# Attention values of a block's four head pairs in one visit, a new plan of feed-forward items, and a new order at the end

## The chip, the cores and the metric

The program runs on one core of a Trainium2 chip. A core has a matrix engine (TensorE, PE in the profile, with PEld for its weight loads), a vector engine (VectorE, DVE), a scalar engine (ScalarE, ACT), GpSimd (POOL) and a queue for transfers (SyncE, SP). The metric is the device time of one execution in microseconds, the median of several; less is better. The profile is of one execution: its span runs from the first to the last instruction of the program.

## What is computed

Top-32 attention over 8 batches of 8 heads (576 tokens, head size 64), whose output goes token by token into a feed-forward network with the activation h·cos h. All in 32-bit floats, except that the two weight matrices arrive as 64-bit floats.

```python
def _attn_ref(q, k, v):                       # (8, 8, 576, 64) each
    scores = np.matmul(q, k.transpose(0, 1, 3, 2)) / np.sqrt(64)
    kth = np.partition(scores, -32, axis=-1)[..., -32:-31]
    scores = np.where(scores >= kth, scores, -1e9)
    attn = np.exp(scores - np.max(scores, axis=-1, keepdims=True))
    attn = attn / (np.sum(attn, axis=-1, keepdims=True) + 1e-09)
    return np.matmul(attn, v)

x = attn_out.transpose(0, 2, 1, 3).reshape(4608, 512)
h = x @ w_in                                  # (4608, 2048)
out = (h * np.cos(h)) @ w_out                 # (4608, 512)
```

## The kernel before

**Units, slots, blocks.** The 4608 tokens are cut into 36 blocks of 128. A block has four units, one for each pair of heads (`hp` 0 to 3), so there are 144 units. A block that straddles two batches (one in nine) has two `parts`, others one. The main loop has one slot for each unit. In slot i VectorE searches the 32 greatest scores of unit i (L303 to L333: eights found by MAX8, struck out by MATCH_REPLACE8); the later stages of earlier units run beside it.

**A unit's way.** Scores: TensorE, L238, into two PSUM buffers `sc` and, for the last 128 keys, into `rim`; two units' scores are made in every even slot. ScalarE copies them out (`take_scores`, L248 from `sc`, L252 from `rim`). One slot after the search its mask (L381) and exponentials (L389) run on ScalarE, from distances `nd` that VectorE has made early in that slot (L340 to L372; ScalarE takes them up at L379). A slot later GpSimd parts the words into halves (`split`, L412, L414), SyncE writes them to DRAM (L440) and reads them back transposed into a `pT` buffer (L446; three buffers). Two slots later still come the values, P@V: `values` (L450) multiplies `pT` with v on TensorE, the last 64 keys first (tails, `v_tail`), into 128 columns of each of the two banks of `rim`. VectorE's `take_values` (L467, the instruction is L473) multiplies the result with the reciprocals of the sums into the block's `xT` (five buffers).

**A visit** is one call of `values` with its `take_values`. Before, each even slot visits two units, those of slots i-4 and i-3: a block takes two visits, 18.64 us apart. In the slot, `take_values` stands inside the last round of the search (L330), so VectorE comes to it some eight microseconds into the slot.

**The feed-forward network** is cut into items that `feed` places between the attention's matmuls. Kind 0, first layer (`ff1`): 16 matmul instructions of 128x128 (L522); a block has 8. Two items fill a PSUM bank `mm` (of two), which ScalarE empties with L536 and L538 (`take_first`); two banks make one `g` buffer, and then GpSimd reduces it modulo a period (L558, L567), ScalarE takes the sine (L577; needs another activation table than the exponential: ACT_TABLE_LOAD) and GpSimd multiplies (`gate`, L584). Kind 1, second layer (`ff2`): 4 instructions of 128x512 (L597); a block has 8, all into one bank `o`, which is also one of the two `mm` banks. ScalarE empties it with L607 and sends it out (`take_second`).

**What sets the order.** The order is written out by hand in `slot` (L700): every engine runs its instructions in the order in which they are issued there. `feed` counts ticks, three in each slot, and skips an item that isn't ready: a first-layer item needs the block's four units taken two ticks ago (L618), a second-layer item its gate three ticks ago (L629). `take_banks` is where ScalarE's emptying of full banks enters its queue. In slot 65 of the kernel before, for example: sine, mask, bank of the first layer, exponentials, `take_scores`, and then L607 of block 13; in slot 66 TensorE's first item is that of block 14 that opens the bank which L607 emptied. `drain` and `forward` (L751 to L778) do what remains after the last slot. The weights are decoded in the first dozen slots, through staging buffers shared with `g` and `x` (`CHUNKS`, L94).

Of the kernel before, what the change touches and what calls it, by code (L numbers as in the profile page):

```python
# [10 lines left out]
F32 = mybir.dt.float32  # L11
# [6 lines left out]
P = 128  # L18
# [12 lines left out]
def kernel(  # L31
# [9 lines left out]
    nc = tc.nc  # L41
    ctx.enter_context(tc.manual_schedule())
    B, H, D, S = qT.shape
    DM, DF = moe_w_in.shape
    NT = S // P
    TAIL = S - NT * P
    MAIN = NT * P
    NP = H // 2
# [6 lines left out]
    consts = ctx.enter_context(tc.tile_pool(name="consts", bufs=1))  # L55
    loads = ctx.enter_context(tc.tile_pool(name="loads", bufs=6))
    work = ctx.enter_context(tc.tile_pool(name="work", bufs=2))
# [32 lines left out]
    for f in range(NF):  # L90
        w = consts.tile([P, DM], F32, tag=f"w_out{f}", name=f"w_out{f}")
        w_out.append(w)
        chunks.append((moe_w_out[f * P : (f + 1) * P, :], w))
    CHUNKS, XB = 7, 3  # L94
    BUSY = range(8, 11)
    ff = {"live": 0, "tick": 0, "now": 0, "end": False, "kind": 0, "half": 0, "open": 0, "late": False}

# [63 lines left out]
    units = []  # L161
    for t0 in range(0, B * S, P):
        parts = []
        for i, a in enumerate((t0, t0 + TAIL)):
            b, q0 = a // S, a % S
# [7 lines left out]
    pairs = {}  # L173
    v_tails = []
    for i in range(2 * NP):
        t = consts.tile([P, P], F32, tag=f"v_tail{i}", name=f"v_tail{i}")
        nc.gpsimd.memset(t, 0.0)
        v_tails.append(t)

    def place(hp, j):  # L180

        return (hp + j) % 2
# [23 lines left out]
    def load_v(b, hp):  # L206
        st = pairs.setdefault((b, hp), {})
        cols = slice(hp * P, (hp + 1) * P)
        t = loads.tile([P, NT, P], F32, tag="v", name="v")
        nc.sync.dma_start(out=t, in_=v[b, 0:MAIN, cols].rearrange("(c p) e -> p c e", p=P))  # L210
        st["v"] = t

        t = st["v_tail"] = v_tails[b % 2 * NP + hp]
        for j in range(2):
            nc.sync.dma_start(
                out=t[place(hp, j) * TAIL : (place(hp, j) + 1) * TAIL, j * D : (j + 1) * D],
                in_=v[b, MAIN:S, hp * P + j * D : hp * P + (j + 1) * D],
            )

# [200 lines left out]
    def turn(u):  # L420

        s = u.pop("s").rearrange("p j k -> p (j k)")
        pT = u["pT"] = work.tile([P, 2 * NT + 2, P], F32, tag="pT", name="pT", bufs=3)
        for half in range(2):
            tt = ps.tile([P, 512], F32, tag="mm", name="tt", bufs=2)
            for c in range(NT):
                at = (half * NT + c) * P
                nc.tensor.transpose(tt[:, c * P : (c + 1) * P], s[:, at : at + P], ident)
            nc.scalar.copy(out=pT[:, half * NT : (half + 1) * NT], in_=tt.rearrange("p (c q) -> p c q", c=NT))
        at = 2 * NT * P  # L430
        nc.tensor.transpose(room[0][:, P : 2 * P], s[:, at : at + P], ident)
        rden = u.pop("rden")
        for j in range(2):
            lhsT = rden[:, j : j + 1].to_broadcast([P, D])
            nc.tensor.matmul(room[1][j * D : (j + 1) * D, P : 2 * P], lhsT, ident, start=True, stop=True)
        nc.scalar.copy(out=pT[:, 2 * NT :], in_=rim[:, :, 3 * P :])
# [4 lines left out]

    def transposes(u):
        rows = u.pop("rows").rearrange("q h k -> (q h) k")
        pT = u["pT"] = work.tile([P, 2 * NT + 2, P], F32, tag="pT", name="pT", bufs=3)
        words = pT.rearrange("p c q -> p (c q)").bitcast(U16)
        nc.sync.dma_start_transpose(  # L446
            out=words.rearrange("p (c q) -> p c q", c=2 * NT + 2), in_=rows
        )

    def values(us):  # L450


        for b, _, rows, r0 in us[0]["parts"]:
            r = slice(r0, r0 + rows)
            for c in (NT, *range(NT)):
                for i, u in enumerate(us):
                    st = pairs[b, u["hp"]]
                    for j in range(2):
                        d, at = slice(j * D, (j + 1) * D), place(u["hp"], j)
                        if c < NT:  # L460
                            lhsT, rhs = st["v"][:, c, d], u["pT"][:, at * (NT + 1) + c, r]
                        else:
                            t = slice(at * TAIL, (at + 1) * TAIL)
                            lhsT, rhs = st["v_tail"][t, d], u["pT"][t, NT, r]
                        nc.tensor.matmul(room[i][d, r], lhsT, rhs, start=c == NT, stop=c == NT - 1)  # L465

    def take_values(us):  # L467
        blk, hp, n = block_of[us[0]["tok"]], us[0]["hp"], len(us)
        if "xT" not in blk:
            blk["xT"] = work.tile([P, NP, P], F32, tag="xT", name="xT", bufs=5)  # L470
        for i, u in enumerate(us):
            to, o, pT = blk["xT"][:, hp + i], room[i][:, 0:P], u.pop("pT")
            nc.vector.tensor_tensor(out=to, in0=o, in1=pT[:, 2 * NT + 1], op=ALU.mult)  # L473
        blk["left"] -= n
        blk["tick"] = ff["tick"]
# [68 lines left out]
    def take_banks():  # L544
        while full:
            take, *what = full.popleft()
            take(*what)
# [92 lines left out]
    def feed(*kinds):  # L640

        ff["tick"] += 1
        for kind in kinds:
            item(kind)

    def feed_any(n):

        ff["tick"] += 1
        for _ in range(n):
# [11 lines left out]
            else:  # L661
                ff["half"] = 1

    scored, last, last_values = {}, {}, {}
    for i, u in enumerate(units):
        two = i % 2 == 0 and 2 < i
        scored.setdefault(i - 2 if two else i - 1, []).append(u)
        for part in u["parts"]:
            last[part[0], u["hp"]] = i - 2 if two else i - 1
            last_values[part[0], u["hp"]] = i  # L670
    at_slot, at_once = {}, {}

    def load_at(i, *what):
        while i in at_slot:
            i += 1
        at_slot[i] = what

    order = [(b, hp) for b in range(B) for hp in range(NP)]
    for n in range(NP, len(order)):
        i = last[order[n - 6]] if n >= 6 else 0  # L680
        load_at(max(i, 2 * NP + 2), load_qk, *order[n])
        i = last_values[order[n - 6]] if n >= 6 else 0
        load_at(max(i + 4 - i % 2, 2 * NP + 2), load_v, *order[n])

    for hp in range(NP):
        at_once.setdefault(hp // 2 + 2, []).append((load_v, 0, hp))
# [7 lines left out]
    def send(x):  # L694

        split(x)
        write_halves(x)
        transposes(x)

    def slot(i, u, w, x, z):  # L700
        n = (3, 4, 4, 4, 4, 3)[i] if i < NP + 2 else 2
        if i < NP:
            for load, b, hp in at_once[i]:
                load(b, hp)
        load_weights(n, nc.sync if i < NP + 2 else nc.scalar)
        if x:
            (turn if i < NP + 2 else send)(x)
        decoding = i < 3 * NP
        ff["late"] = False
        topk_first(u, w)  # L710
        fold_low(u)
        topk_round(u, 1)
        topk_round(u, 2)
        decode_second(NP)
        decode_third()
        reduce_first()
        reduce_second()
        made = scored.get(i, [])
        if z:
            take_banks()  # L720
        feed(0 if i % 2 else 1)

        for m in made:
            scores(m)
        if z:
            values(z)


        if i % 2 or decoding:
            sines(1)  # L730
        if w:
            mask(w)
        take_banks()
        if w:
            exponentials(w)
        if i + 1 < NU:
            take_scores(units[i + 1])
        topk_round(u, 3, both(w), z)
        ff["late"] = True
        if i in at_slot:  # L740
            load, b, hp = at_slot[i]
            load(b, hp)
        gate(1)
        feed(*((1, 1) if i % 2 else (1,)))
        take_banks()
        decode_first(NP)
        reduce_first()
        reduce_second()
        feed(*((0, 0) if i % 2 else (0,)))

    def forward(n):  # L751
        ff["now"] += 1
# [7 lines left out]

    def drain(w, x, z):

        if x:
            send(x)
        if w:
            merge_first(w)
            merge_second(w)
            bounds(w)
            distances(w)
            mask(w)  # L770
            exponentials(w)
            sums(w)
            reciprocal(w)
        forward(2)
        if z:
            values(z)
            take_values(z)
        forward(2)  # L778
# [10 lines left out]
    for i in range(NU):  # L789
        ff["now"] += 1  # L790
        wq["ready"] = wq["done"]
        u, w, x = (units[i - n] if n <= i else None for n in range(3))
        z = units[i - 4 : i - 2] if i % 2 == 0 and i >= 4 else None
        if NP < i < NP + 3:
            z = units[2:4] if i == NP + 1 else None
        slot(i, u, w, x, z)
    ff["end"], ff["late"] = True, False
    drain(units[NU - 1], units[NU - 2], units[NU - 4 : NU - 2])
    drain(None, units[NU - 1], None)
    drain(None, None, units[NU - 2 : NU])  # L800
# [40 lines left out]
```

## Time and profile before

| | |
|---|---|
| time, median of 3 runs | 1440.79 us (1440.24 to 1440.95) |
| the profiled execution, own time | 1440.46 us |
| its span | 1438.7 us |
| 0 to 119 us (start, weights): VectorE, ScalarE, GpSimd busy | 108.87, 92.82, 81.89 of 119.00 us; TensorE's clock 0.67 |
| 119 to 1368 us (regular slots): VectorE, ScalarE, GpSimd busy | 1233.61, 981.80, 1080.41 of 1249.00 us; TensorE's clock 1.00 |
| 1368 to 1438.7 us (end): TensorE, VectorE, ScalarE busy | 62.97, 12.44, 18.83 of 70.70 us |
| an odd slot, start to start on VectorE | 8.99 us |
| an even slot, with its visit | 9.65 us |
| ScalarE's copy of `rim` (L252) waiting for the values (L465) | 93.6 us in 70 waits, longest 3.6 |
| GpSimd's `halves` (L412) waiting for the exponentials | 149.2 us in 68 waits |
| SyncE's transposes (L446) waiting for the written rows | 415.0 us in 137 waits |
| a transpose, issue to landing | 5.0 us |

The profile names, for each group of instructions, the line of the kernel, engine and operation, what is written from what, and how often; then the busy time, the mean of one in nanoseconds, and the idle time ahead of it with what ended that. A timeline has, instead, start, length, engine, line and operation, and in brackets the idle time ahead. Matmuls overlap, so their distance from start to start is what they cost.

### The profile page before, as it was taken

What the parts mean: (1) busy time and instruction counts of PE and PEld (TensorE: products, weight loads), DVE (VectorE), ACT (ScalarE), POOL (GpSimd) and SP (SyncE); (2) the same over time, 40 slices, a digit from 0 to 9 for tenths busy, and PEclk for the clock granted to TensorE, in tenths of its full rate; (3) what the DMA queues carried; (4) which work ended last, traced back from release to release, by engine and by line L of the source; (5) the groups of instructions that cost most, each with busy time, mean ns of one, the idle gap of its engine ahead of it and who ended that gap; (6) DMA issues with size and microseconds to landing.
All of it is one profiled execution on the core that took longest, in us unless ns stands there. A gap on an engine that the chain in (4) does not pass through costs nothing.

```text
span 1438.7 us, 30312 instructions
## 1 busy us (share of the span) xinstructions
PE 1381.0 (96%) x10304; PEld 986.1 (69%) x10304; DVE 1354.9 (94%) x5235; ACT 1093.5 (76%) x1922; POOL 1166.2 (81%) x812
## 2 busy tenths in 40 slices
PE   5578999999999999999999999999999999999988
PEld 3355777777777777777777777777777777777765
DVE  7999999999999999999999999999999999999921
ACT  6967787778777787778777787777777788778722
POOL 4788888888888888888888888888888888888810
PEclk6679999999999999999999999999999999999999
DMA  9576666556655576556665567556765566655530
GB/s 292 186 199 175 186 195 184 148 159 193 189 159 144 167 185 180 162 146 194 187 171 143 143 182 194 166 154 186 185 173 151 150 162 169 160 147 154 155 81 15
DMA packets 427436, 240.01 MB, mean 167 GB/s; under 512 B 375952, under 2 KB 392592, under 8 KB 427280
## 3 DMA queue, kind: packets, MB, share of 16 engines
q1 hardware_dynamic: 420864, 224.75, 57.3%
q10 hardware_dynamic: 6416, 13.32, 2.6%
q8 instruction: 81, 1.33, 0.4%
q14 instruction: 75, 0.61, 0.2%
HBM read 45.09 MB, written 101.19 MB: 102 GB/s over the span
## 4 chain that ended last, share of the span: by engine, by line
PE 90%; DVE 5%; ACT 3%; DMA 1%; POOL 0%; SPq 0%; issue 0%; POOLq 0%
PE o L597 35%; PE mm L522 34%; PE rim L465 11%; PE sc L238 8%; DVE top L352 2%; PE rim L238 2%; DVE rest L357 1%; DMA st<-in_moe_w_in_dram 1%; ACT st L136 1%; ACT s L389 1%; ACT s L381 0%; ACT w_in L133 0%; DMA pT<-rows 0%; DVE low L357 0%; DVE rest L260 0%; DVE w_out L144 0%
## 5 line engine op out<-in xcount | busy, mean ns | idle before, releaser
L522 PEld LDWEIGHTS mm<-xT,w_in 128*128 128x128 f32 x4608 | 538.8, 193 | 70.8 <-issue 66.6
L522 PE MATMUL mm<-xT,w_in 128*128 128x128 f32 x4608 | 539.9, 276 | 4.0 <-ACT x L538 4.0
L597 PE MATMUL o<-w_out,g 128*128 128x512 f32 x1152 | 537.6, 600 | 6.2 <-POOL g L584 6.2
L352 DVE MAX8 top<-rest 128x8 f32<-128x288 f32 x1152 | 478.7, 451 | 0.0
L412 POOL COPY halves<-s 128x2304 uint16<-128x2304 uint16 x140 | 294.7, 2105 | 149.4 <-ACT s L389 149.2
L357 DVE MATCH_REPLACE8 rest<-top,rest 128x288 f32<-128x288 f32 x864 | 376.3, 443 | 0.0
L597 PEld LDWEIGHTS o<-w_out,g 128*128 128x128 f32 x1152 | 203.1, 191 | 194.4 <-issue 187.5
L352 DVE MAX8 top<-low 128x8 f32<-128x288 f32 x576 | 241.7, 448 | 0.6 <-POOL low L285 0.6
L389 ACT ACTIVATE s<-s,nd 128x576 f32<-128x576 f32 x288 | 220.1, 767 | 0.8
L285 POOL TENSOR_TENSOR low<-low,rest 128x576 int32<-128x576 int32 x141 | 200.3, 1420 | 11.0
L381 ACT ACTIVATE s<-s,top 128x576 f32<-128x576 f32 x288 | 206.2, 766 | 0.0
L276 POOL TENSOR_TENSOR low<-s 128x576 int32<-128x576 int32 x141 | 199.3, 1413 | 5.2 <-ACT s L252 5.2
L536 ACT ACTIVATE g<-mm 128x512 f32<-128x512 f32 x144 | 86.0, 598 | 150.6 <-PE mm L522 150.4
L567 POOL TENSOR_TENSOR x<-g,x 128x1024 f32<-128x1024 f32 x68 | 161.5, 2374 | 5.7
L238 PE MATMUL sc<-k,q 64*128 64x448 f32 (+1 forms) x640 | 149.6, 587 | 12.7 <-DMA k<-in_k_dram 7.0
L584 POOL TENSOR_TENSOR g<-g,x 128x1024 f32<-128x1024 f32 x68 | 160.8, 2365 | 0.0
L465 PE MATMUL rim<-pT,v 128*64 128x128 f32 (+1 forms) x2560 | 147.8, 269 | 0.0
L465 PEld LDWEIGHTS rim<-pT,v 128*64 128x64 f32 x2560 | 129.8, 139 | 12.5 <-issue 11.2
L248 ACT COPY s<-sc 128x896 f32<-128x896 f32 x144 | 128.0, 889 | 4.7 <-PE sc L238 4.7
L252 ACT COPY s<-rim 128x256 f32<-128x256 f32 (+1 forms) x160 | 59.2, 370 | 93.8 <-PE rim L465 93.6
L357 DVE MATCH_REPLACE8 low<-top,low 128x288 f32<-128x288 f32 x288 | 125.4, 443 | 0.0
L260 DVE TENSOR_TENSOR rest<-sc,s 128x576 f32<-128x576 f32 x144 | 107.7, 748 | 7.0 <-ACT s L252 6.5
(55 smaller groups left out, 1215.3 us busy)
## 6 DMA issues: line engine op xcount, KB each, us to landing
rows<-halves SPq DMA_DIRECT2D x140, 640.0 KB, 3.0
out_dram<-ob ACTq DMA_DIRECT2D x36, 256.0 KB, 2.0
q<-in_q_dram SPq DMA_DIRECT2D x31, 288.0 KB, 3.5
st<-in_moe_w_in_dram SPq DMA_DIRECT2D x16, 512.0 KB, 7.0
v<-in_v_dram SPq DMA_DIRECT2D x32, 256.0 KB, 3.3
st<-in_moe_w_out_dram SPq DMA_DIRECT2D x9, 512.0 KB, 4.8
k<-in_k_dram SPq DMA_DIRECT2D x31, 144.0 KB, 3.3
k<-in_k_dram SPq DMA_DIRECT2D x32, 128.0 KB, 3.7
```

The costliest lines, as they stand in the source:

```text
L238: nc.tensor.matmul(to[r0 : r0 + rows, rim_bank(r0, j) if k0 else place(u["hp"], j), 0 : k1 - k0], st["q"][d, q0 : q0 + rows], st["k"][d, k ...
L276: nc.gpsimd.tensor_tensor(out=u["low"].bitcast(I32), in0=s[:, :, 0:HS], in1=s[:, :, HS:S], op=ALU.add)
L285: nc.gpsimd.tensor_tensor(out=low, in0=low, in1=u["rest"][:, :, HS:S].bitcast(I32), op=ALU.subtract)
L352: nc.vector.max(to[:, j], src[:, j])
L357: nc.vector.match_replace(rest[:, j], to[:, j], src[:, j], NEG)
L381: nc.scalar.activation(out=s[:, j], in_=s[:, j], func=AF.Prelu, bias=less[:, j, 1:2], scale=1.0, alpha=FAR)
L389: nc.scalar.activation(out=s[:, j], in_=s[:, j], func=AF.Exp, bias=nd[:, j : j + 1], scale=SCALE, accum_out=den[:, j, 0:1],)
L412: nc.gpsimd.tensor_copy(out=halves[:, :, 0 : 2 * S], in_=s.rearrange("p (k h) -> p h k", h=2))
L465: nc.tensor.matmul(room[i][d, r], lhsT, rhs, start=c == NT, stop=c == NT - 1)
L522: nc.tensor.matmul(mm[:, at : at + w], w_in[f // FC][:, c, (f % FC) * P : (f % FC + 1) * P], blk["xT"][:, c], start=c == 0, stop=c == NC - 1,)
L567: nc.gpsimd.tensor_tensor(out=x, in0=g, in1=x, op=ALU.subtract)
L597: nc.tensor.matmul(o, g[:, at : at + P], w_out[f], start=f == 0, stop=f == NF - 1)
```

## The change

- `values` takes all units of a visit into the two banks of `rim`, unit `hp` into bank `hp % 2` at columns `hp // 2 * 128`, and only the first matmul into each bank half sets `start`.
- `value_slot` says when a unit is visited: all four units of a block in the third slot after the block's last (slots 2 modulo 4), but the first two units of a straddling block two slots earlier; the first block in slot 5. `take_values` takes as many units.
- `pT` has five buffers instead of three, `xT` three instead of five, `CHUNKS` is 6 instead of 7, `v_tail` tiles have 64 columns instead of 128 and aren't cleared.
- Items come from a `plan` by slot modulo 4: 2 in the slot of the visit, then 5, 4 and 5 (before: 3 in even slots, 5 in odd ones).
- Loads of v are placed from the slot of the last visit.
- `drain` begins with `take_banks`, and `ff["half"]` is 1 when the end begins.

```diff
-    CHUNKS, XB = 7, 3
+    CHUNKS, XB = 6, 3
@@
-        t = consts.tile([P, P], F32, tag=f"v_tail{i}", name=f"v_tail{i}")
-        nc.gpsimd.memset(t, 0.0)
-        v_tails.append(t)
+        v_tails.append(consts.tile([P, D], F32, tag=f"v_tail{i}", name=f"v_tail{i}"))
@@
-        pT = u["pT"] = work.tile([P, 2 * NT + 2, P], F32, tag="pT", name="pT", bufs=3)
+        pT = u["pT"] = work.tile([P, 2 * NT + 2, P], F32, tag="pT", name="pT", bufs=5)
@@
+    def place_of(u):
+
+        bank, at = u["hp"] % 2, u["hp"] // 2 * P
+        return bank, room[bank][:, at : at + P]
+
     def values(us):
+        begun = set()
         for b, _, rows, r0 in us[0]["parts"]:
             r = slice(r0, r0 + rows)
             for c in (NT, *range(NT)):
-                for i, u in enumerate(us):
-                    st = pairs[b, u["hp"]]
+                for u in us:
+                    st, (bank, to) = pairs[b, u["hp"]], place_of(u)
...
-                        nc.tensor.matmul(room[i][d, r], lhsT, rhs, start=c == NT, stop=c == NT - 1)
+                        nc.tensor.matmul(
+                            to[d, r], lhsT, rhs, start=(bank, j) not in begun,
+                            stop=c == NT - 1 and u in us[-2:] and r0 + rows == P,
+                        )
+                        begun.add((bank, j))
@@
-            blk["xT"] = work.tile([P, NP, P], F32, tag="xT", name="xT", bufs=5)
+            blk["xT"] = work.tile([P, NP, P], F32, tag="xT", name="xT", bufs=3)
@@
+    def value_slot(i, u):
+
+        if i < NP:
+            return NP + 1
+        return i - i % NP + NP + (0 if len(u["parts"]) == 2 and u["hp"] < 2 else 2)
+
+    valued = {}
+    for i, u in enumerate(units):
+        valued.setdefault(value_slot(i, u), []).append(u)
...
-            last_values[part[0], u["hp"]] = i
+            last_values[part[0], u["hp"]] = value_slot(i, u)
@@
-        load_at(max(i + 4 - i % 2, 2 * NP + 2), load_v, *order[n])
+        load_at(max(i, 2 * NP + 2), load_v, *order[n])
@@
+    plan = (
+        ((0,), (1,), (1, 0)),
+        ((0,), (1, 1), (0, 0)),
+        ((1,), (1,), ()),
+        ((0, 0), (1, 1), (0,)),
+    )
@@
-        feed(0 if i % 2 else 1)
+        feed(*plan[i % NP][0])
@@
-        feed(*((1, 1) if i % 2 else (1,)))
+        feed(*plan[i % NP][1])
@@
-        feed(*((0, 0) if i % 2 else (0,)))
+        feed(*plan[i % NP][2])
@@
     def drain(w, x, z):
 
+        take_banks()
@@
-        z = units[i - 4 : i - 2] if i % 2 == 0 and i >= 4 else None
-        if NP < i < NP + 3:
-            z = units[2:4] if i == NP + 1 else None
+        z = valued.get(i)
         slot(i, u, w, x, z)
-    ff["end"], ff["late"] = True, False
+    ff["end"], ff["late"], ff["half"] = True, False, 1
```

## The prediction

> **What bounds the kernel now.** I read the page's busy shares and its chain of waits first, then TensorE's timeline over one pair of slots, then the same stretch on VectorE and ScalarE, then the last 75 us. Shares and chain (both name TensorE):
>
> ```profile
> PE 1381.0 (96%) x10304; PEld 986.1 (69%) x10304; DVE 1354.9 (94%) x5235; ACT 1093.5 (76%) x1922; POOL 1166.2 (81%) x812
> PE 90%; DVE 5%; ACT 3%; DMA 1%; POOL 0%; SPq 0%; issue 0%; POOLq 0%
> ```
>
> TensorE's timeline of one pair of slots (start, length, line; no idle is noted anywhere):
>
> ```profile
> 703.08 1.98 PE L597 MATMUL o<-w_out,g 128*128 128x512 f32 x4
> 704.90 3.73 PE L522 MATMUL mm<-xT,w_in 128*128 128x128 f32 x32
> 708.48 3.60 PE L597 MATMUL o<-w_out,g 128*128 128x512 f32 x8
> 711.91 3.73 PE L522 MATMUL mm<-xT,w_in 128*128 128x128 f32 x32
> 715.48 1.88 PE L597 MATMUL o<-w_out,g 128*128 128x512 f32 x4
> 717.29 1.02 PE L238 MATMUL sc<-k,q 64*128 64x448 f32 x4
> ...
> 719.44 0.45 PE L465 MATMUL rim<-pT,v_tail 64*64 64x128 f32 x8
> 719.82 1.97 PE L465 MATMUL rim<-pT,v 128*64 128x128 f32 x32
> 721.72 1.98 PE L597 MATMUL o<-w_out,g 128*128 128x512 f32 x4
> ```
>
> From start to start (703.08 to 721.72): 18.64 us a pair. An item of the first layer (16 matmuls of L522) is 1.79 us (3.57 for two), one of the second (4 of L597) 1.72; the scores of two units 2.15 (717.29 to 719.44), the values of two 2.28 (719.44 to 721.72). VectorE and ScalarE beside it:
>
> ```profile
> 703.61 0.49 DVE L473 TENSOR_TENSOR xT<-rim,pT 128x128 f32<-128x128 f32 x2 [0.16 <-ACT s L252]
> ...
> 704.92 0.23 DVE L340 TENSOR_REDUCE top<-top 128x34 f32<-128x68 f32 x1
> ...
> 713.91 0.23 DVE L340 TENSOR_REDUCE top<-top 128x34 f32<-128x68 f32 x1
> ```
>
> ```profile
> 706.82 0.20 ACT L379 ACTIVATE nd<-nd 128x2 f32<-128x2 f32 x1 [0.78 <-DVE nd L372]
> ...
> 708.68 0.60 ACT L536 ACTIVATE g<-mm 128x512 f32<-128x512 f32 x1 [0.32 <-PE mm L522]
> ...
> 713.75 0.60 ACT L607 ACTIVATE ob<-o 128x512 f32<-128x512 f32 x1
> ```
>
> What to see: VectorE has no gap but the 0.16 us ahead of L473, where it waits for ScalarE's rim copy (L252), which waited for the values. L340 opens a slot: an odd slot is 8.99 us, and no slot without a multiply waits anywhere. L607 empties the finished bank of the second layer at 714.35; the next block's first L597 takes that bank at 715.48. So TensorE leads, with 1.1 us in hand at this bank.
>
> **What the Trainium skill says.** "TensorEngine Tiling (Array Packing)", Key Properties: changing the tiling mode drains TensorE. The trace agrees: start to start, single matmuls at the changes (scores to tails, tails to main values, values to L597) are 199 to 202 ns apart on the median, where the values' own steps are 7 or 103. "PSUM — Partial Sum Buffer", section on bank collisions: two engines must not touch one bank in the same 32 partitions, whatever the columns. That is why L252 waits for values that it doesn't read (76.0 us over 58 waits in 200 to 1300 us). "TensorE: Matmul & The Clock Gate": ScalarE's queue is strictly first in, first out; and a pause of some 3.4 us halves TensorE's clock. The trace has the second: after a 4.0 us pause at the end, 32 matmuls take 5.26 us instead of 3.73.
>
> **The change, part by part.** Call V the start of the first L597 after a visit, and a group the 37.27 us of four slots.
>
> *The joined visit.* A visit to two units is 2.28 us: tails 0.18, change 0.20, main 1.70, change 0.20. Four units in one: 2x0.18 + 0.20 + 2x1.70 + 0.20 = 4.16, with the joins 4.2. Two visits were 4.56, so TensorE saves 0.35 us a group, and needs 36.92. Scores straight to L597, and L522 straight to scores, are not in the steady trace; the nearest changes cost 0.1 to 0.2 more than no change, so the saving lies between 0.1 and 0.4. It counts only if nothing else sets the group.
>
> *What the visit does to VectorE's place.* VectorE multiplies (L473) at V+0.53, as now, since L252 stands before it in both. Four multiplies are 0.21 each, so the next slot opens at V + 1.84 + 2x0.21 = V+2.26. Two slots of 8.99 follow: slot 1 of the group (mod 4) opens at V+20.24. Its distances reach ScalarE 1.90 later (704.92 to 706.82): V+22.14.
>
> *ScalarE's queue in that slot.* From L379 to the end of L607 now: 714.35 - 706.82 = 7.53, less the 0.31 that L536 waited for TensorE, 7.22, all of it work in order (mask, bank, table, exponentials, two copies, L607). So the bank is free at V+29.36. ScalarE is there in time for the distances: in slot 0 its work ends about V+18.35, and table and sine end near V+20.8, 1.3 us early.
>
> *TensorE reaches that bank.* Between V and the next block's first L597 the new plan has 7 items of the second layer and 8 of the first: 7x1.72 + 8x1.79 = 26.3; scores once, 2.15; changes 0.3. It is there at V+28.75: 0.6 us too early. Now it is 1.1 late, because two units of values stand between on TensorE and VectorE isn't held until four are done. So TensorE stops 0.6 us, plus 0.05 for the signal and 0.05 to start again (0 to 0.15: after a change the first L597 shows 534 ns instead of 429). Behind it on its queue stand the scores and the values. From that L597 to the next V: 1.81 + 2.15 + 4.2 = 8.17. The loop is 29.36 + 0.10 + 8.17 = 37.63 against 37.27: +0.35 a group. It runs through VectorE, ScalarE and TensorE in turn, so the saved drains don't shorten it.
>
> *Groups.* From V at 123.74 (slot 10) to 1355.99 (slot 142) are 33. Four blocks straddle two batches and touch two groups each: in the first, extra scores in slot 0 fall into the stop (+0.16 rather than +0.35), in the second two units stay in a visit of their own, TensorE is 2.4 us later at the bank and nothing waits (0). 25x0.35 + 4x0.16 = +9.4 us.
>
> *Start.* Slots 4 and 8 lose their multiplies (-0.6 and -1.3 with the 0.86 wait), slot 5 has four units at half clock (about +1.9); slot 10 waits for GpSimd's gate (6.2 us) as before, then its visit is 1.9 longer. Sum +1.9; -1 to +6, as the clock of that visit isn't known. One staging buffer less delays one weight chunk by a slot, in slots that wait for VectorE; the eight memsets (1.2 us of GpSimd) lie before any work.
>
> *End.* Now the loop leaves 12 + 20 items, then 13 + 20; the sum of work is the same. The old order stops here:
>
> ```profile
> 1364.82 3.73 PE L522 MATMUL mm<-xT,w_in 128*128 128x128 f32 x32
> 1372.56 5.26 PE L522 MATMUL mm<-xT,w_in 128*128 128x128 f32 x32 [4.00 <-ACT x L538]
> ```
>
> A first-layer item needs a bank whose emptying is queued on ScalarE behind the last units' mask and exponentials. The new order ends the loop with half a bank filled, fills it and goes on in the open second-layer bank, then has the values. By the same durations no later item waits: the closest is the last half of block 35, gated 0.5 us before its use. Gain 4.0 + 1.5, and 0.1 elsewhere: -5.6 (-6.5 to -3).
>
> *At nothing:* five pT buffers (four units held, one being filled; the fifth slot's transpose is issued after the multiplies); later v loads (3 slots in hand, but one as now at the straddling blocks); transposes before the visit (lands near V+30, tails at V+33.4); three xT buffers (one lives 29 us of 37); GpSimd's gates, due slots later (1.6 us in hand). The first L522 at V+1.82 needs xT, ready at V+1.44; a wait there up to 0.6 is swallowed by the stop.
>
> *Sum* on the profiled span: 1438.7 + 9.4 + 1.9 - 5.6 = 1444.4; outside it lie 1.76 (1440.46 - 1438.7): 1446.2. The median shown is 0.33 above the profiled run: 1446.
>
> **Rivals.**
>
> *A, TensorE still leads (faster).* If the bank comes free by V+28.75, the group is 36.92: 25 x -0.35 and 4 x -0.35, -10; with start and end 1440.8 - 10 + 1.9 - 5.6 = 1427. For: every gap on TensorE now is its own, VectorE needs only 36.87. Against: ScalarE's 7.22 is pure work. It decides from 0.6 us less on the way from V to L607.
>
> *B, the sine falls behind (slower still).* In slot 0 the bank is emptied behind the mask, so GpSimd's reduction, the sine and slot 1's mask move later; 1.3 us in hand. Half a microsecond beyond it goes into every ordinary group: 1446 + 12 = 1458. For: GpSimd is 81% busy. Against: its work fits by the durations.
>
> *C, it cancels.* A stop of only 0.3 us (+0.05 a group) and the full end: 1438 to 1442.
>
> **How the numbers follow.** The bank's loop 68%, own range 1440 to 1454 (0.2 to 0.55 a group, with the bounds of start and end); A 15%; B 10%; C 7%. The range 1436 to 1457 holds the first, C and part of B, and leaves out A and the far part of B. No change means within 0.2% (2.9 us), which is what can be told. Faster by more: A and a little of C, 0.17. Within: most of C and a tenth of the likeliest, 0.15. Slower: 0.68.
>
> **What would show it.** Right: an idle of about 0.6 us before L597 once in four slots, put down to ScalarE L607, and a group of 37.6 us; L473's wait grown to about 0.8. At the end no 4 us stop before L522. Wrong: groups of 36.9 with no wait on L597 (A); L379 waiting for the sine and not for nd (B); or the stop before L522 in slot 3, waiting for xT.

## The result, and the profile after

The changed kernel takes 1444.97 us in the median of ten runs (1443.58 to 1449.18), the kernel before, run beside it, 1440.18 (1439.52 to 1441.36): a ratio of 1.0036, 95% interval 1.0026 to 1.0046. So it is slower by 4.8 us, a third of a percent, outside the scatter of both. The profile is of one of these runs, 1449.18 us, with a span of 1447.4; it is the slowest of the ten, and the part on the start says where its 4.2 us above the median lie.

The page, busy shares and chain of waits:

```profile
PE 1374.4 (95%) x10304; PEld 991.8 (69%) x10304; DVE 1351.3 (93%) x5235; ACT 1088.4 (75%) x1922; POOL 1164.8 (80%) x804
PE 41%; DVE 40%; ACT 14%; DMA 2%; issue 2%; POOL 1%; SPq 0%; ACTq 0%
```

TensorE is busy 6.6 us less than before, and the kernel is slower. (Of the 6.6 us only 1.6 lie in the regular slots, from V of slot 10 to V of slot 142; 3.2 lie before them and 1.7 after.) The second line says why that can be: of the chain that ends last TensorE held 90% before and holds 41% now. The bound is no longer one engine but a loop through three. The chain in order of time, from one visit to the next (start, length, what), shows it whole:

```profile
689.96 2.42 PE rim L469 x44
692.41 0.38 ACT s L250
692.81 0.88 DVE xT L481 x4
...
713.94 0.37 DVE top L350
714.60 1.33 ACT s L379 x2
715.93 0.48 ACT g L544
716.41 0.58 ACT x L546
717.01 1.28 ACT L387
718.42 0.56 issue
718.99 0.94 ACT s L387 x3
719.93 0.79 ACT s L246
720.72 0.27 ACT s L250
720.99 0.51 ACT ob L615
721.63 1.96 PE o L605 x4
...
725.74 4.26 PE rim L469 x80
730.02 0.38 ACT s L250
730.43 0.89 DVE xT L481 x4
```

The values (L469, before the change L465) release the copy of `rim`, and that copy releases the multiplies (L481). VectorE then runs two and a bit slots without a gap; its distances release the mask (L379), ScalarE works through its queue to the emptying of the second layer's bank (its eviction: L615, before the change L607), and that releases TensorE's next second-layer item (L605, before the change L597), behind which the next values stand. From multiply to multiply, 692.81 to 730.43, are 37.62 us.

TensorE's timeline of the same four slots:

```profile
692.29 1.98 PE L605 MATMUL o<-w_out,g 128*128 128x512 f32 x4
...
717.48 3.73 PE L530 MATMUL mm<-xT,w_in 128*128 128x128 f32 x32
721.63 1.96 PE L605 MATMUL o<-w_out,g 128*128 128x512 f32 x4 [0.42 <-ACT ob L615]
...
725.67 0.67 PE L469 MATMUL rim<-pT,v_tail 64*64 64x128 f32 x16
726.26 3.71 PE L469 MATMUL rim<-pT,v 128*64 128x128 f32 x64
729.91 1.98 PE L605 MATMUL o<-w_out,g 128*128 128x512 f32 x4
```

The only idle time is the 0.42 us before L605. From start to start the stop is larger: the two first-layer items before it are over at 717.48 + 3.57 = 721.05, so it is 0.58. The regular slots have 25 such stops, and each ends 0.14 to 0.15 us after the end of the eviction L615. Four of them, in the blocks that straddle two batches, the trace puts down to GpSimd's copy L410, which ended 0.03 to 0.04 us before; there too it is 0.14 us from the eviction. VectorE's side, its multiplies at the end of a visit:

```profile
692.81 0.88 DVE L481 TENSOR_TENSOR xT<-rim,pT 128x128 f32<-128x128 f32 x4 [0.77 <-ACT s L250]
...
730.43 0.69 DVE L481 TENSOR_TENSOR xT<-rim,pT 128x128 f32<-128x128 f32 x3 [0.78 <-ACT s L250]
```

VectorE waits 0.78 us a group there (before, 0.16 us in the pair that the prediction shows), so it is not the bound by its own work.

The span in three, by V (the start of the first second-layer matmul after a visit) in slots 10 and 142:

| | before | after | difference | predicted |
|---|---|---|---|---|
| start, to V of slot 10 | 123.74 | 126.11 | +2.4 (see below) | +1.9 |
| 33 groups, V to V | 1232.25 | 1244.28 | +12.0 | +9.4 |
| end, from V of slot 142 | 82.68 | 76.97 | -5.7 | -5.6 |

### The profile page after: what moved, and what is told of

The parts are those of the page before. It is cut to its first block, busy times and chain, and to the rows that moved or that the text cites. A ratio compares the mean times of both kernels' runs of the same rounds, so it can differ in the third digit from the quotient of the medians.

```text
span 1447.4 us, 30339 instructions
## 1 busy us (share of the span) xinstructions
PE 1374.4 (95%) x10304; PEld 991.8 (69%) x10304; DVE 1351.3 (93%) x5235; ACT 1088.4 (75%) x1922; POOL 1164.8 (80%) x804
## 4 chain that ended last, share of the span: by engine, by line
PE 41%; DVE 40%; ACT 14%; DMA 2%; issue 2%; POOL 1%; SPq 0%; ACTq 0%
DVE top L350 19%; PE o L605 14%; PE rim L469 11%; PE mm L530 10%; DVE rest L355 10%; PE sc L236 5%; DVE rest L258 4%; DVE low L355 3%; ACT s L379 3%; ACT L387 2%; ACT s L387 2%; DVE xT L481 2%; ACT s L246 1%; PE rim L236 1%; ACT s L250 1%
## 5 line engine op out<-in xcount | busy, mean ns | idle before, releaser
L605 PE MATMUL o<-w_out,g 128*128 128x512 f32 x1152 | 534.4, 602 | 24.2 <-POOL g L592 10.5
L410 POOL COPY halves<-s 128x2304 uint16<-128x2304 uint16 x140 | 294.8, 2106 | 102.6 <-ACT s L387 98.7
L605 PEld LDWEIGHTS o<-w_out,g 128*128 128x128 f32 x1152 | 205.2, 190 | 230.2 <-issue 210.8
L379 ACT ACTIVATE s<-s,top 128x576 f32<-128x576 f32 x288 | 205.5, 761 | 0.0
L377 ACT ACTIVATE nd<-nd 128x2 f32<-128x2 f32 x144 | 29.3, 204 | 176.1 <-DVE nd L370 176.0
L469 PE MATMUL rim<-pT,v 128*64 128x128 f32 (+1 forms) x2560 | 140.5, 268 | 0.0
L469 PEld LDWEIGHTS rim<-pT,v 128*64 128x64 f32 x2560 | 130.3, 139 | 6.9 <-issue 5.8
```

Of the source, the lines that this page charges most:

```text
L379: nc.scalar.activation(out=s[:, j], in_=s[:, j], func=AF.Prelu, bias=less[:, j, 1:2], scale=1.0, alpha=FAR)
L410: nc.gpsimd.tensor_copy(out=halves[:, :, 0 : 2 * S], in_=s.rearrange("p (k h) -> p h k", h=2))
L469: nc.tensor.matmul(to[d, r], lhsT, rhs, start=(bank, j) not in begun, stop=c == NT - 1 and u in us[-2:] and r0 + rows == P,)
L605: nc.tensor.matmul(o, g[:, at : at + P], w_out[f], start=f == 0, stop=f == NF - 1)
```

## The experiments

Theory: the loop of the bank, as in the prediction. Rivals: VectorE's longer wait at the joined visit sets the group; the uneven plan of items does; ScalarE has simply more to do. Ten kernels, each timed beside the kernel before. "Group" is V to V, read from the matmuls' starts.

**1. The bank emptied earlier.** In slots 1 modulo 4 the eviction goes ahead of the copy of the scores; TensorE's and GpSimd's orders stay.

```diff
+        early = i % NP == 1 and i > 2 * NP
+        if early:
+            gate(1)
+            feed(*plan[i % NP][1])
+            take_banks()
         if i + 1 < NU:
             take_scores(units[i + 1])
...
-        gate(1)
-        feed(*plan[i % NP][1])
-        take_banks()
+        if not early:
+            gate(1)
+            feed(*plan[i % NP][1])
+            take_banks()
```

> The changed kernel, but in slots 1 modulo 4 ScalarE empties the second layer's bank (ob<-o) before it copies the next scores, not after; nothing is left out. Bank theory (the loop runs V, VectorE's slots, ScalarE's queue up to this eviction, TensorE's next second-layer item): the eviction ends 1.05 us earlier, TensorE no longer stops there, a group of four slots falls from 37.62 to 36.9 to 37.05 us, and the time to 1428 to 1433 us. Rival (VectorE's longer wait at the joined visit sets the group): group 37.6, time 1444 to 1446. Rival (the uneven plan 2, 5, 4, 5 sets it): the same, 1444 to 1446.

Measured 1429.31 us, ratio to before 0.9929 (0.9914 to 0.9943). A little over half of the ordinary groups are 36.95 or 36.96, the others 37.05 to 37.2 and one 37.38; 36.92 was what TensorE alone was to need. In its timeline no idle time is left before the item at which TensorE had stopped:

```profile
296.57 3.74 PE L530 MATMUL mm<-xT,w_in 128*128 128x128 f32 x32
300.14 1.88 PE L605 MATMUL o<-w_out,g 128*128 128x512 f32 x4
```

Nothing of the visit or the plan has changed, only what ScalarE does first, and the whole loss in the groups is gone with the stop. Both rivals fall. VectorE's wait at the joined visit (26.6 us in 30 waits between 200 and 1300 us of the changed kernel) is gone as well: it came from the loop and didn't set it.

**2. The same edit in the kernel before.**

> The kernel before with the same earlier eviction in slots 1 modulo 4; nothing is left out. Bank theory: TensorE was 1.1 us late at this bank anyway, so nothing is won: 1440 us; the copy of scores comes 0.6 us later with 0.2 in hand before VectorE's next slot, so up to 3 us may be lost: 1439.5 to 1443. If the earlier eviction were good in itself, it would win 10 us or more here too.

1440.61 us, ratio 1.0007 (0.9998 to 1.0016), groups 37.27 as before. The earlier eviction isn't good in itself: there the bank was free in time.

**3 and 4. A dose on ScalarE, in slot 1 and in slot 0.** One copy is done twice.

```diff
             take_scores(units[i + 1])
+            if i % NP == 1 and i > 2 * NP:        # dose_slot0: == 0
+                again = units[i + 1]
+                nc.scalar.copy(out=again["s"][:, :, 0:SB], in_=again["sc"][:, :, 0:SB])
```

> The changed kernel with the copy of scores out of sc done twice (0.79 us more on ScalarE, same result) in slots 1 modulo 4, ahead of the second layer's eviction. Bank theory: each group that stops at this bank grows by the whole 0.79, 37.62 to 38.4; 28 to 29 groups, 1445 + 23 = 1468 us (1464 to 1471). Rivals (VectorE's wait or the plan sets the group; ScalarE has idle time): under 1450.

> The changed kernel with the same 0.79 us more on ScalarE in slots 0 modulo 4. Bank theory: 1.3 us are in hand between the end of the sine and slot 1's distances, so nothing reaches the loop: group 37.6, 1445 us (1443 to 1448). Rival (ScalarE's sum of work, or the later sine, is what lengthens the group): 1460 or more.

Slot 1: 1473.28 us, ratio 1.0230 (1.0215 to 1.0245), groups 38.43: +0.81, the whole dose. An ordinary stop in this kernel:

```profile
461.18 1.96 PE L605 MATMUL o<-w_out,g 128*128 128x512 f32 x4 [1.23 <-POOL halves L412]
```

The trace names GpSimd's copy L412 in 25 of the 29 stops. It ends within 0.01 us of the item's start there, by coincidence: all 29 stops, these and the four that the trace puts down to L615, end 0.14 to 0.15 us after the eviction, and in the kernel without the dose the same item starts before L412 is over. Slot 0: 1444.74 us, ratio 1.0030 (1.0019 to 1.0042), groups 37.62, as the changed kernel. The same work costs all or nothing by its place; so it isn't ScalarE's sum of work, and the sine has room in slot 0. Slot 1 cost 28 us where 23 were expected. The rest is in three of the four blocks that straddle two batches, whose groups grew by 2.4 to 2.5; TensorE's timeline of the dosed kernel at the first of them, and at the fourth:

```profile
185.33 3.73 PE L530 MATMUL mm<-xT,w_in 128*128 128x128 f32 x32
190.99 3.65 PE L605 MATMUL o<-w_out,g 128*128 128x512 f32 x4 [1.92 <-ACT ob L615]
...
1233.97 1.96 PE L605 MATMUL o<-w_out,g 128*128 128x512 f32 x4 [1.93 <-ACT ob L615]
```

All four stops are 1.92 to 1.93 us. After the first three the granted clock was 0.5 for 3.41 us, beginning 0.05, 0.5 and 1.0 us after the stop's end, and the four matmuls took 3.65, 3.24 and 2.74 us instead of 1.96; after the fourth the clock stayed, and that group grew only by the dose. So a longer stop costs its own length and can then cost clock; the pause of some 3.4 us that the prediction names isn't needed for it.

**5. Two units a visit again**, with plan, buffers and end of the changed kernel.

```diff
-        return i - i % NP + NP + (0 if len(u["parts"]) == 2 and u["hp"] < 2 else 2)
+        return i - i % 2 + 4
```

> The changed kernel with its plan, buffers and end, but two units a visit again (slots 0 and 2 modulo 4). Bank theory: two units of values stand between on TensorE again and VectorE is held only until two are done, so the stop before L605 goes; TensorE needs 37.27 a group: 37.2 to 37.35, and the time 1445 less 12 = 1433 us (1431 to 1436). Rival (the plan or the buffers cost, not the joined visit): 1440 us or more.

1433.27 us, ratio 0.9956 (0.9941 to 0.9970). Groups 37.27 (16.92 + 20.35), 33 of them 1232.17 us: to 0.1 us what they were before the change. So the joining costs the 12 us, and neither plan nor buffers cost anything in the regular slots.

**6. The old plan with joined visits.**

> The changed kernel with the item plan of before (3 in even slots, 5 in odd ones), visits still joined. Bank theory: between V and the next block's first second-layer item stand the same 15 items and one pair of scores, so the stop and the group of 37.6 us stay: 1445 us (1443 to 1448). Rival (the plan 2, 5, 4, 5 sets the group, or is needed for it): a group that differs by over 0.2 us, a time that differs by over 5.

1447.99 us, ratio 1.0058 (1.0043 to 1.0073). Groups 37.62, 33 of them 1244.33: the plan does nothing there. The 3 us are in the end, 80.04 instead of 76.97, a part that I had not thought of for this run: the last slot hands another mixture of items over (see 8).

**7 and 8. The end.** The two lines on the end taken out of the changed kernel, and put alone into the kernel before.

```diff
     def drain(w, x, z):
+        take_banks()
...
-    ff["end"], ff["late"] = True, False
+    ff["end"], ff["late"], ff["half"] = True, False, 1
```

> The changed kernel without the two lines on the end (no take_banks at the head of drain, half not set). If the new order at the end is worth the 5.6 us of the prediction: 1450.6 us (1449 to 1453), with a stop of some 4 us before a first-layer item after the last slot. If the end's gain came from the other parts: 1445.

> The kernel before with only those two lines on the end. Worth 5.6 us: 1434.6 us (1433.5 to 1436.5), no 4 us stop before a first-layer item and no half clock near 1372 us. If the end's gain needs the joined visits or the plan: 1440.

Without them 1452.19 us (ratio 1.0085, 1.0070 to 1.0100), an end of 84.04: 7 us more, with a stop of 3.80 us:

```profile
1382.61 3.54 PE L530 MATMUL mm<-xT,w_in 128*128 128x128 f32 x16 [3.80 <-ACT x L546]
```

Alone in the kernel before 1436.73 (ratio 0.9979, 0.9969 to 0.9988), an end of 80.05: 2.6 us less than in the profile before, half of what was expected (3.1 us by the medians). TensorE's timeline of this kernel's end shows what is left:

```profile
1363.03 3.73 PE L522 MATMUL mm<-xT,w_in 128*128 128x128 f32 x32
1368.03 2.05 PE L522 MATMUL mm<-xT,w_in 128*128 128x128 f32 x16 [1.26 <-ACT x L538]
...
1375.83 1.95 PE L522 MATMUL mm<-xT,w_in 128*128 128x128 f32 x16
1379.04 2.05 PE L522 MATMUL mm<-xT,w_in 128*128 128x128 f32 x16 [1.26 <-ACT x L538]
```

Two stops of 1.26 us where a bank has only just been filled by two first-layer items and the next item is of the first layer too: the plan before ends the loop with a full bank. The new plan's last slot hands over half a bank, and the other item in between gives ScalarE its 1.3 us. The new plan without the two lines makes the end 1.4 us longer than before (84.04 for 82.68), so the end's gain needs both.

**9. The buffers alone**, in the kernel before: five `pT`, three `xT`, six staging buffers, narrow tails.

> The kernel before with only the buffers of the change: five pT, three xT, CHUNKS 6, tails of 64 columns that aren't cleared. Prediction's reading (all of it behind other work): group 37.27, time within 1.5 us of 1440.2. If the smaller staging costs at the start, or three xT buffers cost in every block: over 1442. If more pT buffers win by earlier transposes: under 1438.

1438.77 us, ratio 0.9993 (0.9985 to 1.0002), groups 37.27: nothing that can be told from no change.

**10. A kernel that beats both.** In the kernel of experiment 1 ScalarE still stood between the eviction and the copy, for the transfer of the output waits in its queue for the eviction; and the late copy held VectorE back (10.8 us in 29 waits between 200 and 1300 us). ScalarE's queue in experiment 1:

```profile
298.96 0.57 ACT L615 ACTIVATE ob<-o 128x512 f32<-128x512 f32 x1
299.56 0.34 ACTq L617 DMA_DIRECT2D out_dram<-ob  x1
299.94 0.91 ACT L246 COPY s<-sc 128x896 f32<-128x896 f32 x1 [0.41 <-ACT ob L615]
```

So the transfer is issued after the copies.

```diff
-        nc.scalar.dma_start(out=out[row : row + P, :], in_=ob)
+        ff["out"] = lambda: nc.scalar.dma_start(out=out[row : row + P, :], in_=ob)
+        if not ff["hold"]:
+            ff.pop("out")()
...
             feed(*plan[i % NP][1])
+            ff["hold"] = True
             take_banks()
+            ff["hold"] = False
         if i + 1 < NU:
             take_scores(units[i + 1])
+        if "out" in ff:
+            ff.pop("out")()
```

> The changed kernel with the eviction of the second layer's bank ahead of the copy of the scores (as in early_out), and the transfer of the output issued only after that copy, so that ScalarE doesn't stand 0.4 us between the two. Bank theory: TensorE is the bound there at 36.95 us a group; some groups of early_out were 37.1 to 37.2, because the late copy holds VectorE back 0.37 us in slot 2. They go to 36.95 too: 1 to 3 us less than early_out's 1429.3, 1426 to 1428.5. If VectorE's own work sets those groups: 1429 to 1430.

1424.56 us, ratio to before 0.9893 (0.9878 to 0.9908): 15 us faster than the kernel before and 20 faster than the change. ScalarE now goes straight on, and every ordinary group is 36.95 or 36.96:

```profile
297.85 0.57 ACT L615 ACTIVATE ob<-o 128x512 f32<-128x512 f32 x1
298.33 0.89 ACT L246 COPY s<-sc 128x896 f32<-128x896 f32 x1
298.45 0.34 ACTq L617 DMA_DIRECT2D out_dram<-ob  x1
```

It won 4.75 us on experiment 1, more than the 1 to 3 expected. In the two profiles 3.6 us of the difference are in the groups and 0.55 at the end; the rest lies in the start, where executions of one kernel differ by more than that.

## Why the prediction was right

The forecast was 1446 us, slower; measured were 1444.97. Its steps:

- *The loop.* V to the bank free was to be 29.36: measured 692.29 to 721.49, 29.20 (ScalarE from the distances to the end of the eviction 714.40 to 721.49, 7.09 for 7.22). From there to the item's start 0.10 was booked and 0.14 measured. The stop of 0.6 us is 0.58. From that item to the next V, 8.17 was worked out and 8.28 measured. The group is 37.62 for 37.63. Experiments 1 to 5 show that this loop sets it, and not only that the lengths agree.
- *The joined visit's saving.* 36.92 for TensorE alone, of costs that the trace before didn't hold (scores straight to the second layer, first layer straight to scores): 36.96 where nothing stops it. The saving is real and was worth nothing until the bank came free earlier. Start to start, scores to L605 measure 202 ns, first layer to scores 205 (112 within the first layer, without a change).
- *Straddling blocks.* Here the step failed. "Extra scores in slot 0" were to fall into the stop, and +0.16 was booked. Those groups went from 37.22 to 38.42, +1.20. The term that was left out is ScalarE's: it copies the `rim` of such a unit in two halves, in both kernels, and the prediction took the queue of an ordinary slot for all. ScalarE's timeline in slot 17 of the changed kernel:

```profile
192.20 0.75 ACT L250 COPY s<-rim 64x256 f32<-64x256 f32 x2
192.97 0.60 ACT L615 ACTIVATE ob<-o 128x512 f32<-128x512 f32 x1
```

  From the start of this copy to the start of the eviction are 0.77 us instead of 0.27, and another 0.15 are lost earlier in the queue: the bank is free 29.85 us after V (163.72 in this group) instead of 29.20. From L605 to the next V are 8.43 instead of 8.28. With the 0.14 between them that is 38.42. The scores hardly matter: TensorE reaches the bank at V+28.71 instead of V+28.76, and stands idle for 1.12 us. The groups after these (second straddling group 38.14 for 38.14, the next 37.23) were 0 and -0.05, where 0 and +0.35 were booked. In sum the 33 groups were 12.0 longer, 2.6 more than predicted.
- *The start.* The +1.9 did not come. The profile after has +2.4, but it is an odd one: in slot 10 the tails waited 2.60 us for a transposed buffer, and TensorE's granted clock was 0.5 from 121.5 to 124.9 us, in the middle of the values. In the profiles of the six experiments with joined visits V of slot 10 lies at 121.2 to 122.7, in the four of kernels with the old visits (the kernel before, experiments 2, 8 and 9) at 121.5 to 123.7. Most of this scatter is there before slot 1 opens on VectorE; from that point to V of slot 10 it is 104.2 to 105.0 us with joined visits and 104.5 to 105.1 with the old ones, no difference that can be told. With the groups and the end as measured, the medians of the times leave 123.5 before and 121.9 after, so a small gain isn't excluded. Slot 5 took 10.8 us instead of 10.7, not 1.9 more, for the four units' values took 6.0 us where I had taken half clock throughout. Slots 6 and 7 are 0.7 and 0.4 shorter. They are so in experiment 9 too (10.0 and 9.8 us for 10.7 and 10.2), so the buffers do it and not the visits; which of the buffers wasn't settled.
- *The end.* -5.6 predicted, -5.7 measured (the same old end takes 82.9 and 83.5 in the profiles of experiments 9 and 2, so it may be up to 0.8 more). "The new order ends the loop with half a bank filled" was the step that mattered: experiments 6 and 8 show that the two lines without it win only half.
- *At nothing.* Buffers, transposes, loads and clearing cost nothing that can be told (experiments 5 and 9).
- *Rivals.* A, TensorE still leads, was the right picture of what the change could have been: experiment 1 makes it true, at 1429 where 1427 was worked out. B, the sine, didn't come about: 0.79 us more in slot 0 did nothing, so more than that is in hand. C, that it cancels, wanted +0.05 a group; it is +0.35.

The sum of the groups was 2.6 us too small and the start too large by about 2 us or more. That these nearly cancelled is luck. The loop was right as a mechanism; that its sum met the group to 0.01 us is luck too, for its parts were off by -0.16, +0.04 and +0.11.

## What to carry to other kernels

When two units of work are joined on the engine that leads, ask what that engine's lead was good for: here the two units of values between two other items gave ScalarE the time to empty a bank, and joining them turned 1.1 us in hand into 0.6 too early, 1.7 us of lead, for 0.35 us of saved changes of tiling. Follow each buffer's way round (who fills it, who must be done before it is emptied, who waits for it) and add the lengths; a loop through three engines, each with idle time, can be longer than the busiest engine's work. And before a joined step is given up, look at the queue of the engine that frees the buffer: moving one 0.6 us eviction ahead of the copies of scores, and its transfer behind them, turned +0.4% into -1.1%.

## What was not expected of the hardware

- A transfer issued on ScalarE's queue right behind the eviction that it sends out was followed by 0.41 us of idle time (experiment 1, and the changed kernel itself); issued behind another copy it left none (experiment 10).
- Stops of 1.92 to 1.93 us on TensorE were followed, three times of four, by 3.41 us at half clock, and the four matmuls behind them took 3.65, 3.24 and 2.74 us instead of 1.96 (experiment 3). Stops of 0.42, 1.12 and 1.24 us were followed by 1.95 to 1.96.
- The same start took 126.1 us in the profile of the changed kernel and 121.8 in experiment 7, which differs only at the end. Most of it is a wait of 2.60 us for one transposed buffer, and 1.67 us that the values behind it took longer at half clock (5.38 us for 3.71).
